# Chunked attention with top-1 experts on one core: the routing's Exp earlier, the first loads and turns in another order, the last drain left out

## The chip, the core and the metric

The kernel runs on one core of a Trainium2 chip. The time is that of the device in microseconds (us), from runs of the whole program. A profile records one further execution, instruction by instruction. Engines are called PE (TensorE; PEld is its weight load), DVE (VectorE), ACT (ScalarE), POOL (GpSimd) and SP (SyncE, which here issues loads). L747 is line 747 of the kernel before; in the kernel after, lines past 84 are one higher.

## The reference

Two parts follow one another, all in float32.

```python
# q, k, v: (4, 8, 768, 64); mem_k, mem_v: (4, 8, 8, 64)
for c in range(S // 32):                       # chunk of 32 queries
    l, r = max(0, 32 * c - 16), min(S, 32 * c + 32 + 8)
    k_full = concat([mem_k, k[:, :, l:r]]);  v_full = concat([mem_v, v[:, :, l:r]])
    a = softmax(q_c @ k_full.T / sqrt(64))
    out[:, :, chunk c] = a @ v_full
x = out as (3072 tokens, 512)
logits = x @ w_gate                            # 8 experts
e = argmax(logits);  gate = softmax(logits)[e]
y[token] = gate * (relu(x[token] @ w1[e]) @ w2[e])   # w1 512x1024, w2 1024x512
```

## The kernel before

**Attention, one loop over 32 blocks.** A block is 96 queries (three chunks) of one batch, all eight heads; a batch has eight blocks. Loads of k and q go in pieces of 192 tokens (two blocks, 384 KB each), loads of v by block. All are issued by SP, in the order of the code, into rotating buffers (three for k, three for q, six for v), and SP waits at each load for its buffer. PE turns k and q so that the head's dimension lies on partitions: `turn_k(m)` and `turn_q(m)` each turn half a piece into a tile `tqk`. DVE copies a turned k to `kT` (L645; for the first piece of a batch also the memory keys, L649), ACT a turned q to `qT` (L627). `scores(i)` multiplies them to `sc`, ACT takes the Exp to `ex` (L676), `values(i, g)` multiplies by v to `o` in two halves, and DVE normalizes each half into x (`xr`, L690 and L692). `turn_xb(i)` turns x into `tx`, which ACT copies to `xT` (L699), and `logits(i)` multiplies by the gate's weights; DVE takes the eight logits out (L1065).

The tiles `tqk` and `tx` come from one PSUM pool, `ps_t`, with two buffers that are given out in the order of the code. The code's order is each engine's order, since the loop stands under a manual schedule. In block i it is: scores(i), turn_q(i+2), first half of values(i-1), turn_xb(i-2), logits(i-3), second half of values(i-1), turn_k(i+4).

**Routing, spread over the loop.** Blocks form seven groups, of 6, 6, 5, 5, 4, 3 and 3 blocks. When a group's logits are there, `routed(g)` puts small operations in a list, of which each block takes a few. On DVE they are `top` (L727), `eq` (L731), `weigh` (L734), `first` (L738), `one` (L741, with additions on POOL), and `less` (L746), which subtracts the maximum; `less` also issues the routing's Exp on ACT (L747). Then come sum, reciprocal and labels, one rank product on PE, and the rows to which POOL scatters x (L801). Up to block 23, a block takes up to three of them in one slot and up to five in another.

**Transition.** After 22 blocks, rows of expert 0 are gathered early (two gathers of 128 rows, L880). When the loop is done, work on these 256 rows ("early" pieces: 2 turns `tx0`, 8 products `ph`, 8 half products `py`) is put between the last blocks' turns, logits, ranks and scatters, by hand. Then PE reads eight branch indices from memory.

**Experts.** A planner orders the eight experts' products on all engines with due times. At each expert's end, POOL gets a drain (L1218 is the helper that records it), issued by

```python
        if e > 0:
            op("POOL", one_op(nc.gpsimd.drain))
```

The last expert's stores (`put`, L1275) are indirect writes by POOL to `out`. At the end, `landed()` lets POOL wait for the stores' semaphores (L1574), once in a branch that this input doesn't take and once for the end.

Of the kernel before, what the change touches and what calls it, by code (L numbers as in the profile page):

```python
# [19 lines left out]
B, H, S, D = 4, 8, 768, 64  # L20
# [60 lines left out]
EARLY = 22  # L81
NER = 256
NXR = 12


def window(qb):
# [418 lines left out]
def ordinary(ctx, tc, q, k, v, mem_k, mem_v, moe_w_gate, moe_w1, moe_w2, out, good):  # L505
# [106 lines left out]
    def load_v(i):  # L612
        st[i]["v"] = vs[i % NV]
        load_runs(st[i]["v"][:, :, 0:D], i, window(i % NQB), WIN, v, mem_v)
# [4 lines left out]
            turn(tt[:, a], t[0:n, 2 * a + x], ident[0:n, 0:n])  # L619
        return tt  # L620

    def turn_q(m):
        j, x = divmod(m, 2)
        tq = turned_heads(sbs[j]["qn"], PAIRS, x)
        to = sbs[j]["qT"][D * x : D * x + D, :, x].rearrange("d a (p t) -> d a p t", t=2)
        for t in range(2):
            nc.scalar.copy(to[:, :, :, t], tq[D * t : D * t + D])  # L627

    def turn_k(m):
        j, x = divmod(m, 2)  # L630
        b, s = divmod(j, NSB // B)
        if s == 0 and x == 0:
            turned[b] = apool.tile([128, H // 2, KW], F32, name="kT")
        n = PAIRS + NMEM // 2 if s == 0 else PAIRS
        tk = turned_heads(sbs[j]["kn"], n, x)
        half = turned[b][D * x : D * x + D]
        for t in range(2):
            of = tk[D * t : D * t + D]
            to = half[:, :, 2 * PER * s + t : 2 * PER * s + 2 * PER]
            to = bass.AP(  # L640
                tensor=to.tensor,
                offset=to.offset,
                ap=[list(to.ap[0]), [KW, H // 2], [PER, 2], [QB // 2 + NMEM, 2], [2, QB // 4]],
            )
            i = nc.vector.tensor_copy(to, of[:, :, 0:PAIRS].rearrange("d a (y z p) -> d a y z p", y=2, z=2))  # L645
            keyed.setdefault((b, s), []).append(i.ins.name)
            if s == 0:
                to = half.rearrange("d a (y c) -> d a y c", y=NQB)[:, :, :, QB // 2 : QB // 2 + NMEM]
                nc.vector.tensor_copy(  # L649
                    to.rearrange("d a y (p t) -> d a y p t", t=2)[:, :, :, :, t], bc(of[:, :, PAIRS:], 2, NQB)  # L650
                )

# [65 lines left out]
    def routed(g):  # L718

        t0, t1 = GROUPS[g]  # L720
        n, sl = t1 - t0, slice(t0, t1)
        revs = bc(rev[0:QB], 1, n)
        s = {}

        def top():
            s["top"] = small([QB, n], "ltop")
            nc.vector.reduce_max(s["top"], lgs[g], axis=AX_X)  # L727

        def eq():
            s["eq"] = small([QB, n, E], "eq")  # L730
            nc.vector.tensor_tensor(s["eq"], lgs[g], bc(s["top"], 2, E), op=OP.is_equal)  # L731

        def weigh():
            nc.vector.tensor_tensor(s["eq"], s["eq"], revs, op=OP.mult)  # L734

        def first():
            s["first"] = small([QB, n], "first")
            nc.vector.reduce_max(s["first"], s["eq"], axis=AX_X)  # L738

        def one():  # L740
            nc.vector.tensor_tensor(onehot[:, sl], revs, bc(s["first"], 2, E), op=OP.is_equal)  # L741
            for t in range(t0, t1):
                nc.gpsimd.tensor_tensor(seen[:, t + 1], seen[:, t], onehot[:, t], op=OP.add)

        def less():
            nc.vector.tensor_tensor(lgs[g], lgs[g], bc(s["top"], 2, E), op=OP.subtract)  # L746
            nc.scalar.activation(lgs[g], lgs[g], AF.Exp)  # L747

        def rank():
            rk = s["rk"] = cur["bank"][0:QB, 4 * (D + 1) : 4 * (D + 1) + n * E].rearrange("p (t e) -> p t e", e=E)  # L750
            mm(rk, lhsT=tri[0:QB, 0:QB], rhs=onehot[:, sl], start=True, stop=False)
            mm(rk, lhsT=ones[0:QB, 0:QB], rhs=seen[:, sl], start=False, stop=True)

        def own():
            s["own"] = small([QB, n, E], "own")
            nc.vector.tensor_tensor(s["own"], s["rk"], onehot[:, sl], op=OP.mult)

        def row():
            s["row"] = small([QB, n], "row")
            nc.vector.reduce_sum(s["row"], s["own"], axis=AX_X)  # L760

        def where():
            nc.vector.tensor_copy(dest[:, sl], s["row"])

        def total():
            s["total"] = small([QB, n], "total")
            nc.vector.reduce_sum(s["total"], lgs[g], axis=AX_X)

        def guard():
            nc.vector.tensor_scalar(s["total"], s["total"], 1e-9, None, op0=OP.add)  # L770

        def inverse():
            s["inv"] = small([QB, n], "tinv")
            nc.vector.reciprocal(s["inv"], s["total"])

        def labels(a, e):
            def put():
                nc.vector.tensor_copy(xr[:, a % NXR : a % NXR + e - a, DM + 1], s["inv"][:, a - t0 : e - t0])
                nc.gpsimd.tensor_copy(xr[:, a % NXR : a % NXR + e - a, DM].bitcast(I32), token[0:QB, a:e])

            return put

        puts = []
        for a in range(t0, t1):
            if a == t0 or a % NXR == 0:
                puts.append(("v", labels(a, min(t1, (a // NXR + 1) * NXR))))
        v = [("v", f) for f in (top, eq, weigh, first, one, less)]
        u = [("v", f) for f in (total, guard, inverse)] + puts
        w = [("p", rank)] + [("v", f) for f in (own, row, where)]
        return v + u + w + [("s", lambda t=t: scatter_one(t)) for t in range(t0, t1)]  # L790
# [237 lines left out]
    with tc.manual_schedule():  # L1028
        load_k(0)
        load_q(0)  # L1030
        load_v(0)
        load_k(1)
        load_v(1)
        load_q(1)
        load_k(2)
        load_v(2)
        load_q(2)
        turn_k(0)
        turn_k(1)
        turn_q(0)  # L1040
        turn_q(1)
        for i in range(NB):
            if i % 2 == 0 and i // 2 + 3 < NSB:
                load_q(i // 2 + 3)
            if i % 2 == 1 and (i + 7) // 2 - 1 < NSB and (i + 7) // 2 - 1 >= 3:
                load_k((i + 7) // 2 - 1)
            need(i + 3, load_v)
            scores(i)
            scatter_some(1)
            if i == 0:  # L1050
                turn_k(2)
                turn_k(3)
            need(i + 2, turn_q)
            banks = [ps_o.tile([128, 512], F32, tag="o", name="o") for _ in range(2)]
            cur["bank"] = banks[0]
            routing(1, "p")
            if i >= 1:
                values(i - 1, 0, banks[0])
            routing(5 if i > 23 else 3)
            need(i - 2, turn_xb)  # L1060
            late = logits(i - 3, banks[1]) if i >= 3 else None
            if i >= 1:
                values(i - 1, 1, banks[1])
            if late:
                nc.vector.tensor_copy(*late)  # L1065
            scatter_some(1)
            need(i + 4, turn_k)
            routing(6 if i > 23 else 5)
            hold_back()
            for g in range(len(GROUPS)):  # L1070
                if i - 3 == GROUPS[g][1] - 1:
                    work.extend(routed(g))
            if i == 24:
                fetch_w(0, 4)
            if i >= 24:
                fetch_piece(1)
                fetch_piece(1)
            if len(scatters) >= EARLY and "early" not in cur:
                cur["early"] = i
                early_count(banks[0])  # L1080
                early_gather()
# [11 lines left out]
        room_for_x()  # L1093
        banks = bank_pair()
        values(n - 1, 0, banks[0])
        routing(1, "p")
        scatter_some(1)
        turn_xb(n - 2)
        late = logits(n - 3, banks[1])
# [3 lines left out]
        routing(99, "v")  # L1103
        fetch_w(1, 1)
        fetch_piece(99)
        turn_xb(n - 1)
        banks = bank_pair()
        late = logits(n - 2, banks[1])
        nc.vector.tensor_copy(*late)
        hold_back()  # L1110
        do_early(2)
        scatter_some(1)
        routing(1, "p")
        routing(99, "v")
        hold_back()
# [371 lines left out]
    def expert(e):  # L1487
# [29 lines left out]
        at = {1: [t2[1]], 5: [t2[2], s2[3], s2[2]], 6: [t2[3]] + more[0:1], 2: more[1:2], 7: more[2:3]}  # L1517
        layer(e, A2, w2n, S2, s2n, B2, b2, T2, t2n, ys, yn, False, True, at)
        assert not sends
        if e > 0:  # L1520
            op("POOL", one_op(nc.gpsimd.drain))
        if e + 2 < E:
            get_w(e + 2, 1)
# [42 lines left out]
@with_exitstack  # L1566
def kernel(ctx, tc, *args):
    nc = tc.nc
    gpool = ctx.enter_context(tc.tile_pool(name="gpool", bufs=1))
    good = gpool.tile([1, 1], I32, name="good")  # L1570
    rv, stores = ordinary(tc, *args, good)

    def landed():
        with tc.tile_critical(no_gpsimd_drain=True):  # L1574
            for sem, n in stores:
                nc.gpsimd.wait_ge(sem, n)

    with tc.If(rv == 0):
        landed()
        general(tc, *args)  # L1580
    landed()
# [28 lines left out]
```

## Time and profile before

| | us |
|---|---|
| three runs | 546.52, 545.87, 544.91 |
| median | 545.87 |
| the profiled execution | 544.41 |
| its span, first to last instruction | 542.4 |
| PE busy in it | 509.0 (94%) |
| DVE, ACT, POOL busy | 301.1, 244.7, 155.5 |
| mean granted clock of PE | 0.988 |
| drains at L1218 (7): shortest, median, longest | 2.76, 3.84, 6.14 |

The profiled execution has 2.0 us outside its span, and lies 1.46 us under the median. PE's busy time is modelled at the ends of matmuls, so a gap of a tenth of a microsecond between two of them says little; gaps above that are named in the trace with what released the waiting instruction. A stage is read by the busy time of each engine within its window: the loads' start (0 to 29 us), the loop (to 157), the transition (to 200), the experts (to 528) and the end.

### The profile page before, as it was taken

Reading aid. Unit: us, or ns where it says so; the run is one execution under the profiler, and the core shown is the slowest. Engines: PE = TensorE matmul, PEld = TensorE weight load, DVE = VectorE, ACT = ScalarE, POOL = GpSimd, SP = SyncE. Lnnn points to the kernel's source line nnn. Section 1 sums busy time; section 2 is a strip of 40 time slices with the busy share of each in tenths; the row PEclk is TensorE's granted clock in tenths of the full one; section 3 lists DMA queues with packets and bytes.
Section 4 is the critical chain, followed back from the end, with each engine's and each line's share of the span. In section 5 each row is a group of like instructions: output and inputs, shape, how many; then the busy total and the mean of one; then the engine's idle time right before and its main releaser. Section 6 shows DMA issues by size and latency. Waiting matters only on the chain.

```text
span 542.4 us, 9575 instructions
## 1 busy us (share of the span) xinstructions
PE 509.0 (94%) x3666; PEld 475.4 (88%) x3666; DVE 301.1 (56%) x567; ACT 244.7 (45%) x443; POOL 155.5 (29%) x186
## 2 busy tenths in 40 slices
PE   3889999999989989999999999999999999999991
PEld 2789999999988649999999999987779999999980
DVE  3445666566544517868846457543634777853610
ACT  2446565655632126466553264244215637454311
POOL 2000031313354513526134134212322434412002
PEclk9999999999997999999999999999999999999997
DMA  9999998999992310554615154340415344300002
GB/s 158 173 176 177 156 210 173 206 177 294 283 364 102 95 26 39 188 180 171 219 38 190 39 187 167 109 177 30 181 27 195 118 132 186 79 15 12 1 1 82
DMA packets 81348, 75.01 MB, mean 138 GB/s; under 512 B 39542, under 2 KB 64374, under 8 KB 81280
## 3 DMA queue, kind: packets, MB, share of 16 engines
q1 hardware_dynamic: 71840, 54.60, 41.0%
q0 software_dynamic: 8768, 19.29, 10.8%
q8 instruction: 46, 0.75, 0.6%
q10 hardware_dynamic: 672, 0.18, 0.1%
q14 instruction: 22, 0.18, 0.1%
HBM read 66.13 MB, written 17.50 MB: 154 GB/s over the span
## 4 chain that ended last, share of the span: by engine, by line
PE 81%; issue 9%; DMA 4%; POOL 2%; ACT 1%; DVE 1%; SPq 1%; POOLq 0%; another core or an unknown queue 0%
PE sum_p L511 20%; PE sum_r L511 13%; PE sum_q L511 13%; PE o L511 11%; PE sc L511 7%; PE tqk L516 4%; PE sum_x L516 3%; PE ph L511 3%; DMA kn<-in_k_dram 3%; PE py L511 3%; PE sum_q L516 2%; PE tx L516 2%; POOL out_dram L1275 2%; DMA cst<-c_pack 1%; ACT qT L627 1%
## 5 line engine op out<-in xcount | busy, mean ns | idle before, releaser
L1275 POOL DMA_INDIRECT out_dram<-y,xe x42 | 50.9, 1211 | 181.6 <-PE sum_q L511 62.6
L1292 POOL DMA_INDIRECT xe<-x_dram,rows x35 | 50.6, 1446 | 49.9 <-PE sum_r L511 29.3
L676 ACT ACTIVATE ex<-sc,cst 128x256 f32<-128x256 f32 x96 | 38.4, 470 | 49.9 <-PE sc L511 48.5
L1226 ACT COPY sum_r<-sum_p 128x640 f32<-128x640 f32 x48 | 32.5, 677 | 47.4 <-PE sum_p L511 45.6
L511 PE MATMUL o<-v,ex 128*96 128x65 f32 x512 | 53.9, 249 | 0.0
L511 PE MATMUL sc<-qT,kT 128*128 128x192 f32 x256 | 49.3, 337 | 1.5 <-ACT qT L627 1.5
L511 PEld LDWEIGHTS o<-v,ex 128*96 128x96 f32 x512 | 48.5, 165 | 0.0
L511 PE MATMUL sum_p<-xsT,w 128*128 128x136 f32 (+6 forms) x256 | 47.6, 329 | 0.5
L801 POOL DMA_INDIRECT x_dram<-xr,dest x32 | 30.1, 942 | 59.0 <-PE tqk L516 29.8
L511 PE MATMUL sum_r<-t,w 128*128 128x136 f32 (+6 forms) x256 | 45.8, 326 | 0.0
L511 PE MATMUL sum_p<-t,s 128*128 128x136 f32 (+6 forms) x256 | 45.6, 326 | 0.0
L511 PE MATMUL sum_q<-t,s 128*128 128x136 f32 (+6 forms) x256 | 45.1, 324 | 0.0
L645 DVE COPY kT<-tqk 64x384 f32<-64x384 f32 x64 | 35.5, 554 | 15.6 <-PE tqk L516 14.9
L511 PEld LDWEIGHTS sum_p<-xsT,w 128*128 128x128 f32 x256 | 39.7, 190 | 4.8 <-issue 2.1
L511 PE MATMUL sum_p<-h,w 128*128 128x136 f32 (+6 forms) x256 | 43.8, 324 | 0.0
L511 PEld LDWEIGHTS sc<-qT,kT 128*128 128x128 f32 x256 | 42.0, 195 | 1.9 <-issue 1.4
L511 PEld LDWEIGHTS sum_p<-t,s 128*128 128x128 f32 x256 | 39.7, 190 | 2.6
L511 PEld LDWEIGHTS sum_r<-t,w 128*128 128x128 f32 x256 | 39.6, 190 | 2.6
L511 PEld LDWEIGHTS sum_q<-t,s 128*128 128x128 f32 x256 | 39.8, 190 | 2.3
L511 PEld LDWEIGHTS sum_p<-h,w 128*128 128x128 f32 x256 | 39.5, 190 | 2.3
L1223 DVE TENSOR_TENSOR h<-sum_p,kept 128x640 f32<-128x640 f32 x16 | 13.2, 824 | 48.4 <-ACT sum_r L1226 45.9
L690 DVE RECIPROCAL inv_all<-o 96x4 f32<-96x4 f32 x64 | 11.4, 179 | 48.2 <-PE o L511 43.1
(151 smaller groups left out, 919.3 us busy)
## 6 DMA issues: line engine op xcount, KB each, us to landing
w<-in_moe_w_dram SPq DMA_DIRECT2D x14, 2048.0 KB
kn<-in_k_dram SPq DMA_DIRECT2D x16, 384.0 KB
qn<-in_q_dram SPq DMA_DIRECT2D x16, 384.0 KB
w<-in_moe_w_dram SPq DMA_DIRECT2D x8, 512.0 KB
v<-in_v_dram SPq DMA_DIRECT2D x24, 128.0 KB
v<-in_v_dram SPq DMA_DIRECT2D x24, 112.0 KB
v<-in_v_dram SPq DMA_DIRECT2D x8, 144.0 KB
v<-in_v_dram SPq DMA_DIRECT2D x8, 96.0 KB
```

What stands on the lines that cost most here:

```text
L511: i = nc.tensor.matmul(*args, **more)
L516: i = nc.tensor.transpose(*args)
L627: nc.scalar.copy(to[:, :, :, t], tq[D * t : D * t + D])
L645: i = nc.vector.tensor_copy(to, of[:, :, 0:PAIRS].rearrange("d a (y z p) -> d a y z p", y=2, z=2))
L676: nc.scalar.activation(ex4[:, :, :, sl], sc4[:, :, :, sl], AF.Exp, bias=mask[:, 3 * x + g : 3 * x + g + 1], scale=D**-0.5)
L690: nc.vector.reciprocal(inv, o[:, :, D])
L801: i = nc.gpsimd.indirect_dma_start(out=x_dram, out_offset=bass.IndirectOffsetOnAxis(ap=dest[:, t : t + 1], axis=0), in_=xr[:, t % NXR].bit ...
L1223: op(eng, one_op(lambda: engines[eng].tensor_tensor(out, a, b, op=how)), reads, writes)
L1226: op("ACT", one_op(lambda: nc.scalar.copy(to, of)), reads, writes)
L1275: return nc.gpsimd.indirect_dma_start(out=out, out_offset=bass.IndirectOffsetOnAxis(ap=which.bitcast(I32), axis=0), in_=y, in_offset=None, ...
L1292: return nc.gpsimd.indirect_dma_start(out=x[:, g].bitcast(I32), out_offset=None, in_=x_dram, in_offset=bass.IndirectOffsetOnAxis(ap=rows[: ...
```

## The change

- The routing's subtraction and Exp (`less`) go from sixth to third place in their group.
- The first loads are issued in the order k0 q0 k1 q1 v0 k2 v1 q2 v2 instead of k0 q0 v0 k1 v1 q1 k2 v2 q2, and in the loop k comes at even blocks and q at odd ones, instead of the reverse.
- Of the first turns, k's second is copied by ACT and q's first by DVE.
- Up to block 8 (`SLOW`), turn_k(i+3) comes right after scores(i), ahead of turn_q(i+2), instead of one block earlier at the end of the block. Block 8 has both places. In block 0 this is the same as before.
- In the transition one early piece goes ahead of the last turn of x, which moves behind another; one more early piece in all is done ahead of the next rank; one call that hands out ranks is left out.
- The last expert has no drain.
- SP, not POOL, waits for the stores.

```diff
+SLOW = 8
...
-    def turn_q(m):
+    def turn_q(m, copy=nc.scalar.copy):
...
-            nc.scalar.copy(to[:, :, :, t], tq[D * t : D * t + D])
-
-    def turn_k(m):
+            copy(to[:, :, :, t], tq[D * t : D * t + D])
+
+    def turn_k(m, copy=nc.vector.tensor_copy):
...
-        v = [("v", f) for f in (top, eq, weigh, first, one, less)]
+        v = [("v", f) for f in (top, eq, less, weigh, first, one)]
...
         load_k(0)
         load_q(0)
+        load_k(1)
+        load_q(1)
         load_v(0)
-        load_k(1)
+        load_k(2)
         load_v(1)
-        load_q(1)
-        load_k(2)
+        load_q(2)
         load_v(2)
-        load_q(2)
         turn_k(0)
-        turn_k(1)
-        turn_q(0)
+        turn_k(1, nc.scalar.copy)
+        turn_q(0, nc.vector.tensor_copy)
         turn_q(1)
         for i in range(NB):
-            if i % 2 == 0 and i // 2 + 3 < NSB:
-                load_q(i // 2 + 3)
-            if i % 2 == 1 and (i + 7) // 2 - 1 < NSB and (i + 7) // 2 - 1 >= 3:
-                load_k((i + 7) // 2 - 1)
+            if i // 2 + 3 < NSB:
+                (load_k, load_q)[i % 2](i // 2 + 3)
             need(i + 3, load_v)
             scores(i)
             scatter_some(1)
             if i == 0:
                 turn_k(2)
-                turn_k(3)
+            if i <= SLOW:
+                turn_k(i + 3)
             need(i + 2, turn_q)
...
-            need(i + 4, turn_k)
+            if i >= SLOW:
+                need(i + 4, turn_k)
...
         values(n - 1, 0, banks[0])
-        routing(1, "p")
         scatter_some(1)
         turn_xb(n - 2)
...
         fetch_piece(99)
-        turn_xb(n - 1)
+        do_early(1)
         banks = bank_pair()
         late = logits(n - 2, banks[1])
         nc.vector.tensor_copy(*late)
-        hold_back()
-        do_early(2)
+        do_early(1)
+        turn_xb(n - 1)
         scatter_some(1)
+        do_early(1)
         routing(1, "p")
         routing(99, "v")
         hold_back()
...
-        if e > 0:
+        if 0 < e < E - 1:
             op("POOL", one_op(nc.gpsimd.drain))
...
             for sem, n in stores:
-                nc.gpsimd.wait_ge(sem, n)
+                nc.sync.wait_ge(sem, n)
```

More of the change, by code (lines that the diff above doesn't have):

```diff
@@ L644, in turn_k @@
             )
-            i = nc.vector.tensor_copy(to, of[:, :, 0:PAIRS].rearrange("d a (y z p) -> d a y z p", y=2, z=2))
+            i = copy(to, of[:, :, 0:PAIRS].rearrange("d a (y z p) -> d a y z p", y=2, z=2))
             keyed.setdefault((b, s), []).append(i.ins.name)
@@ L648, in turn_k @@
                 to = half.rearrange("d a (y c) -> d a y c", y=NQB)[:, :, :, QB // 2 : QB // 2 + NMEM]
-                nc.vector.tensor_copy(
+                copy(
                     to.rearrange("d a y (p t) -> d a y p t", t=2)[:, :, :, :, t], bc(of[:, :, PAIRS:], 2, NQB)
```

## The prediction

> **What bounds the kernel now.** I read the page first, then a table by stage, then the waits of PE, then single stretches. From the page, PE's busy tenths in 40 slices of 13.6 us and the granted clock:
>
> ```profile
> PE   3889999999989989999999999999999999999991
> PEclk9999999999997999999999999999999999999997
> ```
>
> PE is full except in the first slices, near slices 12 to 14, and in the last. The same by stage (columns: window, length, then busy us and instruction count of PE, PEld, DVE, ACT, POOL, then granted clock, DMA share, GB/s):
>
> ```profile
> 0.00:29.05 29.05, 15.41 (x104) 13.77 (x105) 11.44 (x27) 10.19 (x21) 3.27 (x17) 1.00 1.11 166
> 29.05:157.00 127.95, 126.33 (x1278) 125.35 (x1279) 77.58 (x274) 74.58 (x175) 27.99 (x58) 1.00 1.01 215
> 157.00:200.00 43.00, 37.86 (x167) 26.64 (x165) 15.44 (x68) 6.79 (x16) 19.75 (x26) 0.92 0.36 121
> 200.00:528.00 328.00, 327.08 (x2106) 308.02 (x2107) 195.89 (x197) 151.08 (x228) 99.88 (x81) 1.00 0.32 111
> ```
>
> There is time to win in 0 to 29 (13.6 us idle), a little in the loop, 5.1 us in the transition, and in the 14.4 us after 528. From 200 to 528 PE works 327.08 of 328 us, and the diff leaves all of it but one instruction at its end. The waits of PE (line, released by: total us, times, longest) and the start of the chain that ended last (start, length, what):
>
> ```profile
> PE tqk L516 <- DMA kn<-in_k_dram: 3.5, 2, 2.3
> ...
> PE tqk L516 <- DVE kT L649: 1.7, 2, 1.0
> ...
> PE tqk L516 <- ACT qT L627: 1.6, 3, 0.7
> ```
>
> ```profile
> 20.60 8.32 DMA kn<-in_k_dram
> 28.92 0.14 issue
> 29.05 0.52 PE tqk L516 x4
> 29.57 1.33 PE sc L511 x8
> 30.90 0.33 PE tqk L516 x4
> 31.23 0.65 PE o L511 x8
> 31.89 0.34 PE tx L516 x4
> ```
>
> The start is bound by loads: k3's turn (29.05) stands behind a transfer that landed at 28.92. After it, PE goes from operation to operation with no gap. One of the loop's three stalls, in the timeline (start, length, operation, in brackets the idle time before it and its releaser):
>
> ```profile
> 61.77 0.20 DVE L746 TENSOR_TENSOR lg<-lg,ltop 96x48 f32<-96x48 f32 x1
> ...
> 62.00 0.24 ACT L747 ACTIVATE lg<-lg 96x48 f32<-96x48 f32 x1 [2.33 <-DVE lg L746]
> 62.15 1.17 ACT L676 ACTIVATE ex<-sc,cst 128x256 f32<-128x256 f32 x3
> ...
> 64.27 0.55 PE L516 MATMUL tqk<-cst,kn 96*128 96x96 f32 x4 [0.45 <-ACT qT L627]
> 64.85 1.12 DVE L645 COPY kT<-tqk 64x384 f32<-64x384 f32 x2 [0.29 <-PE tqk L516]
> ```
>
> ACT stands 2.33 us at routing's Exp; the score Exp and the qT copies behind it come late, and PE waits for them.
>
> [...] nothing passes the Exp above. [...] clock 0.50 from 163.78 to 170.61, twice 3.41 us, behind a stretch where PE was idle. [...] In the trace the two early gathers, issued at 155.75 and 157.16 beside 2 MB weight loads, landed 6.2 and 6.1 us later, against 2.1 to 4.3 at 186 to 195.
>
> **The change, part by part.** Minus is time won.
>
> *Start.* k3 now goes ahead of q3 and v3 on SP, 393 KB and about 250 KB. At the 166 GB/s of the first row these are 2.4 and 1.5 us, so I estimate that k3 lands at 25.2, not 28.92. k1 and q1 also no longer stand behind the constants' load (its wait was 1.2 us), and turns 0 and 1 no longer wait for one engine's eight copies (the 1.7 us above): block 0's scores move from 12.51 to about 11.7, which is then hidden behind later loads. Turn 6 (k3's first half) was ahead of block 3's scores and is now behind them. If it runs at 25.3 it does so with 1.33 us of scores already done: 3.7 + 1.33 = **-5.0**. That block 2 is done in time: q2, estimated at 21.4 (22.59 before), lets its turn start at 21.5, and tqk .33, o .65, tx .34, o .65, sc 1.33 end at 24.8. Later loads (q3 at 29.0, k4 32.8, by the same rate) come before their use.
>
> Against it stands a new wait. Turns of q, k and x share a PSUM pool of two buffers. Before, a block's order was q, x, then k at its end, so x took the buffer of a k turned 2.3 us earlier. Now, in blocks 2 to 8, it is k, q, x: x takes the buffer of the k of its own block and waits for its copies. From the timeline: turn at 64.27, copies from 64.85 to 65.97, thus 1.70 after the turn's start; with some .08 to wake PE, 1.78. PE gets there after .33 + .34 + .65 = 1.32. Stall .46. Queued behind it on PE is the rest of the block: nothing covers it, as PE bounds. Block 2 waits for q2 anyway; blocks 3, 4, 7, 8 pay 4 x .46 = 1.84. Blocks 5 and 6 turn the next batch's first keys, with two more DVE copies (L649, .27 each): about .97 each, 1.94. Sum **+3.8** (bounds 0, if DVE's copies come sooner, and the rival's below). The start nets **-1.2**.
>
> *Exp third.* The three blocks with a stall took 4.99 (59.83 to 64.82), 4.99 (86.78 to 91.77) and 5.27 (109.40 to 114.67) us against 4.32 to 4.33 of their neighbours: .66 + .67 + .94 = **-2.27**. With its subtraction third on DVE, the Exp comes a slot earlier, when ACT is ahead of the xT copy instead of ahead of the score Exp; it delays xT by .24, and xT's reader is more than that later. The weigh that yields its place runs in the next slot, ahead of the rank that needs it. Bounds -2.3 to -1.0.
>
> *Transition.* One piece of the early expert's work is put ahead of the last x turn, and one more piece of each kind ahead of the point where PE reads its branch indices. There the trace shows a .80 gap at 190.75, ahead of a py; two matmuls more now stand before it: **-0.8** (0 to -1.5). The idle 3.0 us from 159.64 to 165.84 remain by my count: PE now reads the gathered rows first, which landed at 161.97, where its next operation waited until 162.21 anyhow, for DVE, which itself waited 1.6 us for a queue that the profile doesn't name. The half clock I take as unchanged; its two windows cost 6.83/2 = 3.4 us. The last q load moves behind two w pieces on SP: used four blocks later, nothing. POOL's queue is the same here.
>
> *End.* Behind y's last copies POOL stands in a drain, which began at 528.02 and took 3.97 us; the next put started at 532.83, though y2 was ready at 531.00. A put follows its y by .27, so 1.56 us of the puts' chain go, of which POOL's own sequence (532.06 to about 531.04) gives 1.0. The waits on the stores (539.50 to 540.80 on POOL, SP then waiting 1.4 for it) move to SP, which is free from 537.10: some .5. Together **-1.5** (-0.5 to -2.5). Behind SP's new wait only the end is queued. The six other drains (2.76 to 6.14 us) stay.
>
> *Copies shared* are counted in the start. Routing's call that is removed had nothing in its queue there: nothing.
>
> Sum: -1.2 - 2.27 - 0.8 - 1.5 = **-5.8**; I take off .4, because three of the four terms' bounds reach further toward less: **-5.4**. The profiled execution took 544.41 (span 542.4 and 2.0 around it), which would be 539.0; it is 1.46 under the median, 545.87, and on that scale I say **540.5**. A measurement of this kernel tells about 0.3%, 1.6 us, from no change.
>
> **Rivals.** *Slower:* the two-buffer wait. It decides once x waits 9.2 us in all (3.8 + 5.4), 1.3 per block over seven blocks. That is so if each k's copies start only behind DVE's normalizing (.18 + .42, twice) instead of right away: .46 + 1.2 = 1.66, x7 = 11.6, **548.3**. For it: DVE is in order and already 60% busy in the loop. Against it: its normalizing comes .65 or more after the turn. *Stall hidden:* PE's waits for x cost nothing, the start gives 5.0: 540.5 - 3.8 = **536.7**. For it: blocks 5 to 8 could have other slack; against: the loop's 126.33 busy of 127.95. *Clock kept:* [...] the half clock's 3.4 us go: **537.1**. For it: three idle stretches of .24 to 2.5 us[...]; against: their sum is unchanged. *It doesn't do what it says:* the first loads are bound by bytes, the order only shifts which one is late, the start gives no 5.0 and the stalls stay: 540.5 + 5.0 = **545.5**, no change.
>
> **How the numbers follow.** Forecast .45 (its own range 538.3 to 543), stall hidden .17, clock kept .20, these all faster; loads only shifted .09, same; buffer wait .09, slower. Both middle gains at once reach 533. The range 535.2 to 545.0 leaves out that pair and the slower end. Faster .82, same .09, slower .09.
>
> **What would show it.** k3 landing near 25 and its turn near 25.3; in blocks 3 to 8, PE waits of tx for kT of DVE, about .46 and twice about 1; no wait of PE for qT behind L747; no half clock, or two windows of it, near 163; no drain after 520, and the last put about 1.5 us nearer to the last matmul. Wrong it is if tx doesn't wait at all in blocks 3 to 8, or if k3 lands after 27.

## The result, and the profile after

| | before | after |
|---|---|---|
| median of 20 runs (us) | 545.71 | 540.12 |
| lowest to highest | 543.5 to 548.2 | 536.75 to 545.64 |
| ratio, with 95% interval | | 0.9894 (0.9877 to 0.9911) |

The change makes the kernel 5.8 us faster (4.9 to 6.7). The ratio leaves out three slow executions of the 20 after the change (545.14 to 545.64, mean granted clock 0.976 to 0.979). The first of them is the one that was profiled first, so the profile is read from a second one of the same kernel, `a_repeat`: 538.17, span 536.3. The line numbers of all kernels with the whole change are one higher than before.

From its page, PE's busy tenths and the granted clock:

```profile
PE   3889999999999989999999999999999999999992
PEclk9997999999999999999999999999999999999998
```

And the table by stage (window, length, busy us of PE, PEld, DVE, ACT, POOL, then clock, DMA share, GB/s):

```profile
0.00:29.05 29.05, 18.52 (x134) 17.05 (x134) 12.57 (x29) 12.48 (x28) 3.27 (x17) 1.00 1.12 164
29.05:157.00 127.95, 125.01 (x1223) 123.50 (x1223) 75.08 (x269) 71.63 (x167) 28.01 (x58) 0.97 1.00 226
157.00:196.00 39.00, 37.06 (x194) 26.64 (x193) 15.81 (x70) 8.37 (x20) 19.88 (x26) 1.00 0.31 97
```

The first 29 us hold 3.1 us more PE work than before (18.52 against 15.41; 134 matmuls recorded against 104), at about the same rate of the loads (164 against 166 GB/s). But the loop, with the three Exp stalls gone, is less full than before: 125.01 of 127.95, where it was 126.33. What it waits for is new (waits of PE: line, releaser, total us, times, longest):

```profile
PE tx L517 <- DVE kT L646: 1.6, 5, 0.3
PE tx L517 <- ACT qT L628: 1.0, 1, 1.0
```

The waits of tqk for DMA and for ACT's qT, shown before, are not among them any more. The half clock behind the transition is absent in this execution; instead 6.83 us of it stand at 39.93, in slice 4, shortly behind the wait of 1.0 for ACT's qT.

### The profile page after: what moved, and what is told of

Its sections match the earlier page's. It is cut to its first block, busy times and chain, and to the rows that moved or that the text cites. A ratio compares the mean times of both kernels' runs of the same rounds, so it can differ in the third digit from the quotient of the medians.

```text
span 543.4 us, 9599 instructions
## 1 busy us (share of the span) xinstructions
PE 517.6 (95%) x3666; PEld 484.1 (89%) x3666; DVE 300.0 (55%) x565; ACT 246.0 (45%) x445; POOL 156.2 (29%) x186
## 4 chain that ended last, share of the span: by engine, by line
PE 83%; issue 9%; DVE 3%; POOL 2%; DMA 1%; ACT 1%; POOLq 0%; SPq 0%
PE sum_p L512 20%; PE sum_r L512 13%; PE sum_q L512 13%; PE o L512 12%; PE sc L512 8%; PE tqk L517 4%; PE sum_x L517 3%; PE ph L512 3%; PE tx L517 3%; PE py L512 3%; PE sum_q L517 2%; DVE kT L646 2%; POOL out_dram L1276 2%; DMA kn<-in_mem_k_dram 1%; ACT qT L628 0%
## 5 line engine op out<-in xcount | busy, mean ns | idle before, releaser
L512 PE MATMUL o<-v,ex 128*96 128x65 f32 x512 | 56.6, 256 | 0.0
L512 PE MATMUL sc<-qT,kT 128*128 128x192 f32 x256 | 53.1, 355 | 1.4 <-ACT qT L628 1.1
L512 PEld LDWEIGHTS o<-v,ex 128*96 128x96 f32 x512 | 51.4, 173 | 0.0
L512 PEld LDWEIGHTS sc<-qT,kT 128*128 128x128 f32 x256 | 45.0, 206 | 1.9 <-issue 1.4
L646 DVE COPY kT<-tqk 64x384 f32<-64x384 f32 x62 | 34.4, 554 | 20.9 <-PE tqk L517 20.3
```

Of the source, the lines that this page charges most:

```text
L512: i = nc.tensor.matmul(*args, **more)
L646: i = copy(to, of[:, :, 0:PAIRS].rearrange("d a (y z p) -> d a y z p", y=2, z=2))
```

## The experiments

All were compared with the kernel before in five rounds. Times given as "less" or "more" are the ratio times the median of before in the same comparison. Block times are the distances between the first products of successive `scores`.

**a_repeat**: no edit.

> The kernel after, once more. Both theories expect about 540 us, 1.0% under the kernel before. Wanted is its profile: in the one above, the PE clock was halved at 43.07 and 138.64 inside the loop. If the clock theory holds (the half-clock windows in the loop come and go from one execution to the next), this profile shows another number of them, and its span moves by some 1.7 us for each window of 3.41 us. If the waits alone set the time, the block times of blocks 3 to 8 are the same as above (4.85, 4.85, 5.61, about 5.3 without a half clock, 4.85, 5.19) and nothing else in the loop is over 4.7.

Measured 538.97, ratio 0.988 (0.9856 to 0.9904). Blocks 3, 4, 7, 8 took 4.85, 4.85, 4.85, 5.19, as in the first profile. Blocks 5 and 6, with the half clock over them, took 6.34 and 6.95. But block 26 took 5.97, which the waits named in the expectation don't explain; `b_less` does. The half-clock windows were other ones than in the first profile (3.41 us at 43.07 and 6.83 at 138.64 in the loop there, 6.83 at 39.93 here), so both theories hold something: the waits are the kernel's, and where a half clock comes differs by execution.

**b_start**: the kernel before with the start alone (loads, shared copies, k turned early up to block 8).

> The kernel before with the start alone: the loads' order, the shared copies and the early turns of k up to block 8. As I predicted it, the start nets -1.2: 544.5. By the profile of the kernel after, block 9's scores start at 59.09 instead of 55.35, of which 1.7 is one half-clock window: the start then costs 2.0, 547.7, and the rest of the change must bring about 7.6. Rival that the start is worth most of the gain: 541.

Measured 545.54, ratio 1.0001 (0.9987 to 1.0014): nothing, between my two numbers. Its chain of waits (start, length, what), blocks 3 and 5:

```profile
26.78 0.35 PE tqk L517 x4
27.14 0.55 DVE kT L646
27.71 0.57 DVE kT L646
28.42 0.52 PE tx L517 x4
...
37.16 0.67 PE o L512 x8
37.83 0.47 ACT qT L628
38.31 0.50 ACT qT L628
38.85 0.55 PE tx L517 x4
```

The chain leaves PE and goes through the copies of the k that was just turned. A piece of a chain begins where the one before it ends by the model, so lengths from the start of an operation are read from the timeline:

```profile
26.61 0.49 PE L517 MATMUL tqk<-cst,kn 96*128 96x96 f32 x4
...
28.42 0.52 PE L517 MATMUL tx<-cst,xr 96*128 96x96 f32 x4 [0.33 <-DVE kT L646]
```

x's turn comes 1.81 after the start of k's, instead of the 1.32 that PE's own work takes. In block 5 the chain goes through q's copies on ACT, and x comes 2.53 after k (36.32 to 38.85). Blocks 3 to 8 took 4.85, 4.85, 5.61, 5.27, 4.85, 5.19, of which .34 in block 8 is the second k turn that it holds; without it they are 4.4 more than six blocks of 4.32. Block 3's scores start at 25.26 (29.41 before; 29.20 to 31.26 in the other five profiles with the old start), block 9's at 55.88 (55.35 before). What the loads won is spent by block 9.

**a_slow0**: the turns put back, the rest of the change kept.

```diff
-SLOW = 8
+SLOW = 0
```

> The kernel after with SLOW = 0: the turns of k stand at the end of the block as in the kernel before, all else of the change stays. Theory (x waits for a buffer that the k turn of its own block holds): the waits of tx for kT go, blocks 3 to 8 take 4.3 to 4.7 again, 4.0 to 5.0 us less: 535.5 to 536.5. Rival (the turns were moved because k's pieces land late, and put back they wait for the load): k4 to k7 turn too early, PE waits for DMA kn by as much as the tx waits were, and the time stays at 539 to 541.

Measured 535.0, ratio 0.9801 (0.9774 to 0.9828), 4.3 less than `a_repeat` beside it. Blocks 3 to 8 took 4.32 to 4.33, and no wait of PE for DMA kn is left but that for the first piece. The rival falls: k's pieces land early enough for the old places.

**a_xlate**: k stays early, x comes later.

```diff
-            need(i - 2, turn_xb)
+            if i > SLOW:
+                need(i - 2, turn_xb)
...
             if i >= 1:
                 values(i - 1, 1, banks[1])
+            if i <= SLOW:
+                need(i - 2, turn_xb)
```

> The kernel after, but up to block 8 the turn of x stands behind the second half of values instead of ahead of the logits; k's early turn stays. x then comes 1.97 us after the k turn's start instead of 1.32, and k's copies are done at about 1.78. Theory of the buffer wait: no wait of tx in blocks 2, 3, 4, 7, 8, some 0.3 us left in 5 and 6 (four copies), 3.5 to 4.3 us less: 536 to 536.5. Rival (the early turn itself delays the score Exp and the q copies, whatever the buffer): PE waits in the same blocks at another instruction, and the time stays within 1 us of the kernel after, 539 to 541.

Measured 535.59, ratio 0.9804 (0.9784 to 0.9825). Blocks 3 to 7 took 4.34 to 4.36, and of the seven waits of x on k's and q's copies one is left:

```profile
PE tx L517 <- DVE kT L646: 0.2, 1, 0.2
```

Two different edits, one that takes k's turn away from x and one that takes x away from k's turn, remove the same 4 us. The buffer shared by the two is the cause, not the early turn by itself.

**b_less**: the Exp third, and nothing else.

> The kernel before with the routing's subtraction and Exp third, and nothing else. As predicted: the three stalls go, -2.27, so 543.4. The rival comes from the profiles of the runs with the whole change: block 26 takes 5.98 there and 4.66 before, because the one-hot, now sixth, falls out of its block's slot and the rank right behind it waits for it and for POOL's additions (.33 and .86). Then the gain is 2.27 - 1.32 = 0.95: 544.8, with 4.32 in blocks 10, 16 and 21, and 5.98 in block 26.

Measured 544.74, ratio 0.9983 (0.9967 to 0.9998), .9 less: the rival's number. Blocks 10, 16 and 21 took 4.32, 4.32 and 4.33, so the three stalls did go. Block 26 took 5.99, 4.66 before. Its timeline:

```profile
132.26 0.20 DVE L741 TENSOR_TENSOR onehot<-cst,first 96x40 f32<-96x40 f32 x1
132.51 0.36 PE L511 MATMUL o<-onehot,cst 96*96 96x40 f32 x2
132.54 1.30 POOL L743 TENSOR_TENSOR seen<-seen,onehot 96x8 f32<-96x8 f32 x5 [3.63 <-DVE onehot L741]
133.62 0.36 PE L511 MATMUL o<-seen,ones 96*96 96x40 f32 x2 [0.75 <-POOL seen L743]
```

The one-hot has slid to sixth. In this group the first slot holds five operations, so it runs in the next one, right ahead of the rank on PE, which waits for it and then for POOL's five additions. Block 30 took .23 more than before (4.28 against 4.05), so the block times give 2.26 - 1.33 - .23 = .7 of gain.

**c_best**: `a_slow0` with the Exp third in the first three groups only.

```diff
-        v = [("v", f) for f in (top, eq, less, weigh, first, one)]
+        order = (top, eq, less, weigh, first, one) if g < 3 else (top, eq, weigh, first, one, less)
+        v = [("v", f) for f in order]
```

> The kernel with SLOW = 0, and the routing's Exp third only in the first three groups, sixth in the others, as before. Theory (the one-hot must stay in the slot ahead of the rank): block 26 takes 4.66, 1.3 less than with Exp third everywhere: 533.7. Rival (the late Exp of these groups stalls the score Exp again, as in the loop): 535 or above.

Measured 534.7, ratio 0.9788 (0.976 to 0.9816), which cannot be told from `a_slow0`. Block 26 took 4.66 and block 31's scores began at 148.29 instead of 149.68, so the loop gave the expected 1.4. The rival's stall isn't there: blocks 27 to 30 took the times of before. In the profiled executions the gain was given back behind the loop: the gathers were issued no earlier (150.33 against 150.38), so PE's wait for the gathered rows rose from 1.17 to 2.12, and the half clock that followed lasted 13.65 us against 6.83. The profiled one was the longest of c_best's six (538.9), so what the others lost isn't shown.

**b_trans**: the transition's order alone.

> The kernel before with the transition's order alone. As predicted -0.8: 544.9. By the profiles of the whole change the stretch from block 31's scores to the first expert product is 43.3 to 44.7 with a half clock in it, against 47.0 before: -2.3 to -3.7, about 542.7; and 40.4 without the half clock. If the gain of that stretch belongs to the other parts (an earlier start, the Exp), this stays at 545.

Measured 543.51, ratio 0.9952 (0.9937 to 0.9967), 2.6 less, the second number. PE's timeline of the kernel before, and then of this one:

```profile
159.96 0.39 PE L516 MATMUL tx<-cst,xr 96*128 96x96 f32 x2 [0.32 <-issue]
162.21 0.39 PE L516 MATMUL tx<-cst,xr 96*128 96x96 f32 x2 [1.87 <-DVE xr L692]
...
163.93 1.11 PE L516 MATMUL tx<-cst,xe 128*128 128x128 f32 x4 [0.24 <-issue]
...
165.84 0.51 PE L511 MATMUL o<-seen,ones 96*96 96x24 f32 x2 [0.60 <-issue]
```

```profile
162.04 0.96 PE L516 MATMUL tx<-cst,xe 128*128 128x128 f32 x4 [1.99 <-DMA xe<-x_dram,rows]
...
163.99 1.09 PE L516 MATMUL tx<-cst,xe 128*128 128x128 f32 x4
164.88 0.85 PE L516 MATMUL tx<-cst,xr 96*128 96x96 f32 x4
165.76 2.50 PE L511 MATMUL ph<-x0T,w 128*128 128x256 f32 x5
```

Four waits (.32, 1.87, .24, .60) have become one of 1.99: x's last turn stands behind the gathered rows, when DVE has long finished it, and an early product stands ahead of the rank while POOL adds. The .80 gap ahead of py is gone too. That is 1.04 + .80 = 1.8 of the 2.6; the other .8 is not shown in the trace, and 1.8 is the edge of the interval.

**b_tail**: no last drain, and SP waits for the stores. **b_drain** and **b_spwait**: each alone.

> The kernel before without the last expert's drain and with the waits on the stores on SP, and nothing else. As predicted -1.5: 544.2. By the profiles of the whole change the stretch from PE's last sum to the last put is 3.04 instead of 4.59, and from there to the end 6.5 to 6.6 instead of 7.04: -2.0, 543.7. If the drain only moves its wait to the put behind it, the put still starts 1.28 after the one before and the time is 545.3.

> The kernel before without the last expert's drain, and nothing else. If the prediction's terms hold, the puts start 1.56 earlier and POOL's own sequence gains 1.0: 544.4. By the profile of b_tail the stretch to the last put is 1.55 shorter and the last landing is moved with it: 543.8. If the time saved by b_tail (2.7) is mostly the drain's, 543.0.

> The kernel before with the last waits on the stores on SP instead of POOL, and nothing else. As predicted .5: 544.9. By the profile of b_tail, where the stretch from the last put to the end is 6.07 against 7.04, up to 1.0: 544.4. If POOL's end is what the program's last barrier waits for anyhow, nothing: 545.4.

Measured: b_tail 542.65, 0.9944 (0.9923 to 0.9965), 3.1 less; b_drain 544.55, 0.9964 (0.995 to 0.9978), 2.0 less; b_spwait 545.42, 0.9995 (0.998 to 1.001), which is no difference that can be told. The drain is most of it. The puts of before, and then of b_drain, in the timeline:

```profile
529.00 0.98 POOL L1275 DMA_INDIRECT out_dram<-y,xe  x1 [0.30 <-issue]
532.83 0.98 POOL L1275 DMA_INDIRECT out_dram<-y,xe  x1 [2.85 <-ACT y L1262]
```

```profile
528.57 0.98 POOL L1275 DMA_INDIRECT out_dram<-y,xe  x1 [0.30 <-issue]
530.84 0.98 POOL L1275 DMA_INDIRECT out_dram<-y,xe  x1 [1.29 <-ACT y L1262]
```

POOL's pause between these two puts falls from 2.85 to 1.29, by the 1.56 that was forecast, and from PE's last sum to the last put it is 3.03 instead of 4.59. From there to the end it is 7.02 (7.04 before): what the puts win the end wins whole. With SP's waits alone that last stretch is 6.67, with both in b_tail 6.07; in the other profiles with SP's waits it is 6.45 to 7.06, without them 7.01 to 7.08. So b_tail's trace shows 1.55 + .97 = 2.5 of its 3.1.

**d_gather**: `c_best`, and expert 1's weight loads held until the early gathers are issued.

```diff
+    def hold_w():
+        fetch_w(1, 1)
+        for name in ("w1", "w2"):
+            nc.gpsimd.memset(ms[1][name][0:1, 0, 0:1], 0.0)
...
-            spread.append(lambda g=g: gather(xe0[:, g], rows0[:, g : g + 1], EARLY))
+            spread.append(lambda g=g: (gather(xe0[:, g], rows0[:, g : g + 1], EARLY), g and hold_w()))
...
-        fetch_w(1, 1)
         fetch_piece(99)
```

> The kernel of c_best, but the two 2 MB loads of expert 1's weights must wait for a one-element write that POOL does behind the two early gathers, so they no longer run beside them. Theory (the gathers are late because they share the DMA engines with these loads, and PE's gap ahead of the gathered rows is that lateness): they land 2.1 to 4.3 us after their issue instead of 6.2 and 6.3, the gap of 2.1 us goes, and the time falls by about 2 to 532.7, or by up to 5 where a half clock goes with it. Rival (the gathers take 6 us by themselves): the gap stays, 534.7. Second rival: expert 1's weights come too late, and the first of its sums wait for them.

Measured 533.18, ratio 0.9747 (0.9715 to 0.978). The gathers landed 3.6 and 4.0 us after their issue, against 6.3 and 6.2 in c_best. They were also issued 1.6 us earlier (148.75 against 150.33), which the expectation did not foresee: POOL first waits for the last scatters, and the one issued at 141.83 in c_best landed at 149.33, the same one here, issued at 142.45, at 145.20. PE's waits from 150 to 170 us, of c_best and then of this kernel:

```profile
PE tx L517 <- DMA xe<-x_dram,rows: 2.1, 1, 2.1
```

```profile
PE tx L517 <- ACT x0T L1000: 1.0, 1, 1.0
```

The wait for the gathered rows is gone; half as much is left, for a copy behind the Exp of the last routing. The second rival isn't there either: none of PE's listed waits is for expert 1's weights. That the loads delayed the gathers, and the scatters ahead of them, is shown by the trace. That the kernel is faster than c_best is likely (2.2 by the two ratios) and not settled, as the intervals overlap.

**e_start**: `d_gather` with SLOW = 1, and k1's first turn ahead of the first scores.

```diff
-SLOW = 0
+SLOW = 1
...
         turn_q(1)
+        turn_k(2)
         for i in range(NB):
...
-            if i == 0:
-                turn_k(2)
```

> The kernel of d_gather with SLOW = 1 and the turn of k1's first half moved ahead of the first scores, so that scores 0 and 1 need no turn that waits for k2 (which lands at 16.7) and none for copies that begin only after scores 0. x is not turned before block 2, so the early turn of block 1 holds no buffer that x wants. Theory (the start is bound by PE's own cold chain, turn, copy, scores, until k3 lands at 24.5): scores 1 start some 1 to 2 us earlier than 17.9, scores 3 at about 25.3 instead of 26.6 to 27.0, and the time falls by about 1.3 to 532. Rival (k3's landing and q2's at 20.6 bind): scores 3 at 26.6 or later, 533.2. [...]

Measured 530.55, ratio 0.9732 (0.97 to 0.9764), the fastest of all. Block 1's scores start at 16.40 (17.88 in d_gather) and block 3's at 25.88 (26.98), 1.1 of the 1.3 and not the rival's 26.6. The clock differs too: d_gather has a half clock from 18.43 to 21.85 (a turn's four products took .52 at 16.36, .85 at 19.95 and .50 at 22.52), e_start its first full clock at 19.72 (.78 at 19.12, .49 at 19.75) and no half clock in the loop or the transition, which a single profile can't credit to the edit. By the two ratios e_start is .8 faster than d_gather, and the intervals overlap, so the gain is not settled.

## Why the prediction was right, and where not

The forecast was 540.5, and 540.12 was measured. That the sum came so close is luck: of its four terms two were too large, by 1.2 and 1.4, and two too small, by 1.8 and 1.6.

| | forecast | measured alone, less (-) or more (+), with interval |
|---|---|---|
| start | -1.2 | 0.0 (-0.7 to +0.8), b_start |
| Exp third | -2.27 | -0.9 (-1.8 to -0.1), b_less |
| transition | -0.8 | -2.6 (-3.4 to -1.8), b_trans |
| end | -1.5 | -3.1 (-4.2 to -1.9), b_tail |
| sum | -5.8, taken as -5.4 | -6.6; the whole change -5.8 (-6.7 to -4.9) |

*Start.* The mechanism that I set against the gain is the one that acts, and two edits that remove it confirm its size: 3.8 forecast, 4.4 in the block times, 4.3 by a_slow0. In the short blocks x comes 1.81 after the start of k's turn, where 1.78 was forecast (PE starts .14 behind the end of k's last copy, 28.28 to 28.42 in b_start, where .08 was my estimate), and the block is .53 longer instead of .46; blocks 5 and 6 cost 1.29 and .95 instead of .97 each, block 5 because x waits there for ACT's q copies. The gain was sized wrong. k3 landed where I put it or earlier (23.74 in b_start, 25.15 in a_repeat, 25.2 forecast, though 28.92 - 2.4 - 1.5 is 25.0), but its turn came at 26.61 in b_start, not 25.3. The step that failed is "block 2 is done in time": with q2 no longer late, block 2 was bound by PE's own line of turn, copy and scores, and it paid the buffer wait itself. That makes 2.4 + 1.33 = 3.8, not 5.0.

*Exp third.* The three stalls went, as counted. The step that failed is the sentence on the operation that yields its place: I said that weigh runs in the next slot, ahead of the rank that needs it, and counted that at nothing. It is the one-hot, last of the six, that crosses the slot's border, in one group only, and there the cover is missing: 1.33 of the 2.27 went to block 26, and .23 to block 30.

*Transition.* The .80 is right. "The idle 3.0 us remain by my count" is the step that failed: I took it that PE would wait for the gathered rows as long as it had waited for DVE, and left out that the later waits (.24, .60) would then lie behind work. b_trans has 1.99 in place of 3.03. (The prediction counts three idle stretches of .24 to 2.5; the timeline has four, the longest 1.87.)

*End.* The drain's 1.56 is right in the trace. The step that failed is the reduction to the 1.0 of POOL's own sequence: the end follows the puts, not POOL's instructions, so the whole 1.56 counts. What SP's waits add (forecast .5) is .4 in the trace of b_spwait, 1.0 in that of b_tail, and lies within the noise of b_spwait's time. b_tail's 3.1 may be too large by its draw: its seven executions had a median clock of 0.990, those of before beside them 0.982.

*Rivals.* "Stall hidden" is out: the stall is there. "Slower" named the right place but would have needed 1.3 us a block; it was .53, with 1.29 and .95 in two. "Loads only shifted" is out, as PE got 3.1 us more work into the first 29. "Clock kept" is not settled. The transition of a_repeat's profile has no half clock, but that of the first profile after the change has 6.83 us of it, as before. Over all executions the mean granted clock is higher after the change: its median is 0.9885 in the 20, and 0.982 in the 28 of before that ran beside b_less. I estimate from this .0065 x 540 = 3.5 us of lost clock less. Some of it lies behind PE's last matmul, where it costs nothing and where the profile of before has 6.6 us of half clock and that of a_repeat 4.9, so that half of the difference, .8 of the 3.5, is no gain. Up to some 2.7 of the 5.8 may thus be fewer half clocks, and no run separates them from the waits.

## What to carry to other kernels

Moving one user of a rotating buffer moves the wait of the next user: before a turn is moved, write down who takes its buffer next and what must be copied by then. An operation moved forward in a list that is served in slots pushes the last one out of its slot, so look at the last one and who reads it. And a sum that comes out right can hold errors of both signs: only the parts run alone showed that the early turns cost 4 us that the change could have kept.

## What the runs showed of the hardware

The half clock at the same place of the same program, or of one that differs elsewhere, had no fixed length: none in a_repeat's transition, 3.41 us in d_gather's, 6.83 in before's, 10.24 in b_less's and b_start's, 13.65 in c_best's, which is one to four times 3.41. Under it, the eight products of a block's scores took 2.82 us instead of 1.49 (first profile after the change, at 141.19 and 134.01). By estimate from the granted 0.50, each 3.41 costs up to 1.7 us, as much as most terms of this prediction.

The start differed too. The trace's first record of a granted clock, a full one, begins at 17.01 us in before and at 22.59 in the first profile after the change. Ahead of it none is recorded, and the tables show 1.00, but PE was slower there: in before, the four products of a turn took .88 at 10.47 and .49 at 20.73, the eight of a block's scores 2.90 at 12.51 and 1.49 at 19.41.

The prediction has PE idle ahead of its half clock. PE was not idle throughout: it was busy for 1.48 of the 3.41 us ahead of the one in before's transition, for 2.37, 2.52 and 3.08 ahead of the three in the first profile after the change (43.07, 138.64, 165.95), and for 2.38 ahead of the one in a_repeat's loop. Of these, before and a_repeat (PE's busy time is the number behind the comma):

```profile
160.37:163.78 3.41, 1.48 (x14) 1.24 (x14) 1.76 (x11) 0.49 (x3) 3.24 (x3) 1.00 0.98 368
```

```profile
36.51:39.93 3.42, 2.38 (x29) 2.24 (x26) 2.11 (x6) 2.43 (x6) 0.00 (x0) 1.00 1.10 173
```

The three half clocks in the loops of the two profiles after the change (43.07, 138.64, and 39.93 in a_repeat) begin within 2.3 us of the end of a wait that the change made: block 5's for ACT's q copies (1.04) or block 26's ahead of the rank (.75). a_xlate's loop has one too, at 132.65. Whether such a wait brings a half clock, and so costs more than its length, is not shown: b_start has the first of these waits, b_less and a_slow0 the second, without a half clock there.

I had counted the half clock as a fixed cost of the transition's idle time. That was my assumption, and no run shows what sets the half clock's length. In c_best's profile it lasted 6.83 us longer than in a_slow0's, 3.4 us of time by the same estimate, and beside that the 1.4 us won in the loop of c_best can't be seen.
